# A preamble rebuilt: idle products on TensorE, another order of loads, four weight tiles read where they are converted, scans in halves

## The chip, the cores and the metric

The kernel runs on one core of a Trainium2 chip. Its engines take their own instruction lists in order and wait for each other by semaphores: TensorE (PE in the profile, its weight loads PEld), VectorE (DVE), ScalarE (ACT), GpSimd (POOL) and SyncE (SP), which issues most DMAs. The metric is device microseconds from start to end of one execution, lower is better. The kernel before takes 944.94 us (median of three runs, 944.64 to 945.94).

## The reference

```python
# attention: per batch b and head h a 48x48 state, over 768 time steps
cur = u * k[t] outer v[t];  y[t] = r[t] @ (state + cur)
state = w[t][:, None] * state + k[t] outer v[t]
# x: (4*768 tokens) x 384
h = x @ moe_w_in;  x = (h * clip(h + 3, 0, 6) / 6) @ moe_w_out            # 2048 hidden
xn = x / sqrt(mean(x*x) + 1e-6) * rms_g
out = (silu(xn @ moe2_w_gate) * (xn @ moe2_w_val)) @ moe2_w_out          # 1536 hidden
```

Everything is float32.

## The kernel before

The time axis is cut into 6 chunks of 128 steps, so a chunk has 4 x 128 = 512 tokens. A job is one chunk of one batch (24 jobs); within a job the recurrence is turned into products over 128 steps. The kernel is one stream of steps: for each chunk and each of the 16 tiles of 128 hidden columns ("layers", f) there is one step with a product into the hidden layer (hps, `ff1`), a relu on ACT and a minimum and multiply on DVE (g, `emit_act`), and, one step later, a product back to 384 columns (o, `ff2`). For chunk 0 the first five layers run twice, on columns 0 to 255 of the tokens (jobs 0 and 1) and then on 256 to 511 (jobs 2 and 3), so that jobs 2 and 3 can be made meanwhile: steps 0 to 4 are layers 0 to 4 on the first half, step 5 is layer 0 on the second.

A job of chunk 0 goes through these pieces (methods of `Job`):

- `scans` on DVE: two scans over w (the two halves of the tile), with a reciprocal between them. `muls`: r and k multiplied by what the scans give (rk).
- `pairs` on DVE makes rp, `pe_bonus` multiplies it with u (tile uc) on PE into cps, ACT copies it to cb; `fill` on ACT writes eight tiles a, iperm scaled by cb.
- `pe_a` on PE: the scores aps from rk. `choose` on DVE: where the mask says so, a takes the scores.
- `pe_y0` on PE: yps from v and a; `copy_y0` on ACT puts it into x0, the input of the layers.
- `pe_kt`, `copy_kt`, `pe_u`, `add_u` bring the state up to the next chunk (ktp by transposes with ident, ups, st).

The input weights are stored as 64-bit floats. A `Weight` (one layer's two matrices) is loaded as raw, ACT makes mag from the upper words (`scale`), DVE shifts the lower words (`TENSOR_SCALAR x<-raw`) and joins both (`x<-mag,x`) into a tile x (`bits`), and a DMA copies x to its place in the arena wide_a. For tiles 0 and 1 (`near`) layer products of the first half read x itself; for all others they read wide_a, so they wait for that DMA. raw, x and mag rotate through 3, 3 and 2 buffers; the load of tile f+3 waits until raw f has been read.

The order of work is written by hand. Ahead of the steps a preamble issues the loads and runs jobs 0 and 1 whole and parts of job 2 and of tiles 0 and 1 (the calls of `run` at the end of the set-up). In the steps, the lists `before`, `between` and `behind` say what is issued ahead of a step's first product, between its two products, and after. Each engine takes its instructions in this order; SP does so for DMAs, which move in one queue over 16 DMA engines, and at most eight are issued ahead of the oldest that has not landed, since there are eight DMA semaphores in turn.

Of the kernel before, what the change touches and what calls it, by code (L numbers as in the profile page):

```python
# [28 lines left out]
W1 = 7  # L29
# [7 lines left out]
def kernel(  # L37
# [23 lines left out]
    ps_h = pool(pctx, "ps_h", 2, space=PSUM)  # L61
    ps_s = pool(pctx, "ps_s", space=PSUM)
# [24 lines left out]
    dd = a1_p.tile([128, NP, 2, HF + 1], F32, name="dd")

    st_all = [a1_p.tile([128, 16 + NP * D + 16], F32, name=f"st{b}") for b in range(B)]
    st = [t[:, 16:16 + NP * D].rearrange("p (a d) -> p a d", a=NP) for t in st_all]  # L90
    uc = a1_p.tile([128, NP, 2], F32, name="uc")
    f1 = [a1_p.tile([128, NP, 1], F32, name=f"f1{b}") for b in range(B)]

    def arena(p, name, n):
# [37 lines left out]
    class Weight:  # L132
# [16 lines left out]
        def bits(self):  # L149
            x = st_p.tile([128, 2 * DM], U32, tag="x", name="x", bufs=3)  # L150
            nc.vector.tensor_scalar(x, self.words()[0], 29, None, ALU.logical_shift_right)
            nc.vector.scalar_tensor_tensor(
                out=x, in0=self.mag.bitcast(U32), scalar=3, in1=x, op0=ALU.logical_shift_left, op1=ALU.bitwise_or)
            self.x = x.bitcast(F32).rearrange("p (a n) -> p a n", a=2)
            nc.sync.dma_start(
                out=self.dst[:, :, 1, :].bitcast(U32), in_=x.rearrange("p (a n) -> p a n", a=2))
            if not self.near:
                self.x = self.dst[:, :, 1, :].bitcast(F32)

# [8 lines left out]
    class Piece:  # L168
# [31 lines left out]
        def out(self):  # L200
            hl = de_p.tile([128, 2 * DM], F32R, tag="hl", name="hl", bufs=3)
            h = hl.rearrange("p (l n) -> p l n", l=2)
            nc.scalar.activation(out=h[:, 0, :], in_=self.x, func=AF.Copy)
            nc.gpsimd.tensor_tensor(out=h[:, 1, :], in0=self.x, in1=h[:, 0, :].bitcast(F32), op=ALU.subtract)
            dst = wo_d[self.s] if self.kind == 2 else wp_d[self.j]
            nc.sync.dma_start(out=dst[:, self.f], in_=h.bitcast(F32))
# [57 lines left out]
    class Job:  # L264
# [16 lines left out]
                out=x, data0=x, data1=dd.rearrange("p a h j -> p (a h j)"),  # L281
                initial=0.0, op0=ALU.mult, op1=ALU.add)

        def scans(self):
            nc.vector.memset(dd[:, :, :, 0:1], 1.0)
            self.scan(0)
            self.s1, self.s2 = self.w[:, 0], self.w[:, 1]
            nc.vector.reciprocal(out=dd[:, :, :, 0:1], in_=self.s1[:, :, :, HF:HF + 1])
            self.scan(1)

        def decay(self):
            b = self.b
# [150 lines left out]
            nc.scalar.activation(out=x0[:, :, self.b * CH:(self.b + 1) * CH], in_=self.yps, func=AF.Copy)  # L443


    def emit_h(slot, xt, ps):
        for k in range(KT):
            for j, (l, r) in enumerate(PASS):
                nc.tensor.matmul(  # L449
                    ps, slot[:, l, k * 128:(k + 1) * 128], xt[:, k, r, :],  # L450
                    start=(k == 0 and j == 0), stop=(k == KT - 1 and j == 2))
# [83 lines left out]
    jobs = [Job(c, b) for c in range(NC_) for b in range(B)]  # L535
    wa = [Weight(wa_d[f]) for f in range(F1)]
# [9 lines left out]
    before, between, behind = ([[] for _ in steps] for _ in range(3))  # L546
# [14 lines left out]


    j0, j1, j2, j3 = jobs[:B]
    before[0] += [j2.muls]
    between[0] += [j3.pairs, j2.pe_bonus, j2.fill]
    between[1] += [j2.pe_a, j2.choose, j3.pe_bonus]
    behind[1] += [wa[3].scale, j3.fill, j2.pe_y0, j2.copy_y0, j3.scans]
    before[2] += [j3.muls]
    behind[2] += [j3.pe_a, j3.choose]
    between[3] += [j3.pe_y0, j3.copy_y0]  # L570
    for j, n in enumerate((1, 2, 3, 4)):
        behind[n] += [jobs[j].decay]
        behind[n + 1] += [jobs[j].pe_kt, jobs[j].copy_kt]
# [4 lines left out]
        for b in range(B):  # L578
            plan(c * B + b, first[c] - 18 + 4 * b)

    begun = {f: f - 2 for f in range(2, W1)} | {7: 7, 8: 8} | {f: f + 1 + (f > 13) for f in range(9, F1)}
    for f, n in begun.items():
        if n != 1:
            (behind[n - 1] if n else before[n]).append(wa[f].scale)
        behind[n] += [wa[f].bits]
        if f + 3 < F1:
            behind[n] += [wa[f + 3].load]
    for f in range(F1):
        before[f + 19 if f < F32_F else f + LAGS[0] - 1] += [wa[f].parts]
    behind[2] += [lambda: jobs[4].load("w", "rk", "rks", "v")]  # L590
    behind[4] += [lambda: jobs[5].load("w", "rk", "v")]

    def norm_plan(c, n, last):
# [59 lines left out]
    def run(fs):  # L653
        for x in fs:
            x()
# [297 lines left out]
        return [lambda m=m: one(m) for m in range(KT)]  # L953


    j0.load("w")
    nc.vector.memset(uc, 0.0)
    for i in range(2):
        nc.sync.dma_start(
            out=uc[64 * i:64 * i + D, :, i], in_=u_d.rearrange("o (p i d) -> i d (o p)", p=NP, i=2)[i])  # L960
    j0.load("rk")
    j1.load("rk")
    nc.sync.dma_start(out=iperm, in_=iperm_d)
    j1.load("w")
    nc.sync.dma_start(out=mask, in_=mask_d)
    wa[0].load()
    j0.load("v")
    j1.load("v")
    j2.load("w")
    wa[1].load()  # L970
    j2.load("rk")
    j3.load("rk", "w")
    wa[2].load()
    j2.load("v")
    j3.load("v")
    nc.sync.dma_start(out=ident, in_=ident_d)
    nc.sync.dma_start(out=ub, in_=u_d.to_broadcast([128, DM]))
    nc.sync.dma_start(out=gain, in_=g_d)
    nc.vector.memset(dd, 0.0)
    nc.vector.memset(half, 0.5)  # L980
    nc.vector.memset(eps, 1e-6)
    nc.vector.memset(ones.bitcast(F32), 1.0)
    for t in st_all:
        nc.gpsimd.memset(t, 0.0)
    for f in range(W1):
        wa[f].dst = wpair[f]
        wa[f].near = f < 2
    run((j0.scans, j0.pairs, j0.pe_bonus, j0.muls, j1.pairs, j0.fill, j0.pe_a, wa[0].scale, j1.pe_bonus, j1.fill))
    run((j1.scans, j1.muls, lambda: j1.pe_a(True), j0.choose, j0.pe_y0, wa[0].bits, wa[3].load, j1.choose, j1.pe_y0))
    run((wa[1].scale, wa[1].bits, wa[4].load, j2.pairs, j2.scans, j0.copy_y0, j1.copy_y0))  # L990
    pin()


# [40 lines left out]
    ps_h = pool(ctx, "ps_h1", space=PSUM, reuse_waits="tile")  # L1034
# [106 lines left out]
    for j in range(6 * NG + 1):  # L1141
        p, k = divmod(j, 2 * NG)
# [34 lines left out]
        want, n = {5: 7, 6: 6}.get(j, 9), 0  # L1177
# [107 lines left out]
```

## Time and profile before

| | |
|---|---|
| median of three runs | 944.94 us (944.64 to 945.94) |
| the profiled execution, own time | 944.94 us |
| its span, first to last instruction | 943.1 us |
| PE busy | 927.3 us, 98% |
| DVE, ACT, POOL busy | 644.2 (68%), 476.1 (50%), 534.8 (57%) |
| PE's first product | at 8.70 us |
| HBM read and written | 134.29 and 39.32 MB |
| share of the chain of waits | PE 92%, DVE 3%, DMA 2%, issue 1%, ACT 1%, POOL 1% |

The profile is that of one execution. An engine is busy while an instruction of it runs; what it did ahead of an instruction, and what it waited for, stands in square brackets behind a row of the timeline ("idle before, released by"). The chain of waits is followed back from the last instruction: at each point it names the one thing that was being waited for. Products on PE are in pairs of records where the operands are float32. A granted clock of 1.00 is 2.4 GHz, 0.50 is 1.2; where the trace has no record of it the column shows 1.00.

### The profile page before, as it was taken

Reading aid. Unit: us, or ns where it says so; the run is one execution under the profiler, and the core shown is the slowest. Engines: PE = TensorE matmul, PEld = TensorE weight load, DVE = VectorE, ACT = ScalarE, POOL = GpSimd, SP = SyncE. Lnnn points to the kernel's source line nnn. Section 1 sums busy time; section 2 is a strip of 40 time slices with the busy share of each in tenths; the row PEclk is TensorE's granted clock in tenths of the full one; section 3 lists DMA queues with packets and bytes.
Section 4 is the critical chain, followed back from the end, with each engine's and each line's share of the span. In section 5 each row is a group of like instructions: output and inputs, shape, how many; then the busy total and the mean of one; then the engine's idle time right before and its main releaser. Section 6 shows DMA issues by size and latency. Waiting matters only on the chain.

```text
span 943.1 us, 14286 instructions
## 1 busy us (share of the span) xinstructions
PE 927.3 (98%) x5085; PEld 733.9 (78%) x5085; DVE 644.2 (68%) x913; ACT 476.1 (50%) x946; POOL 534.8 (57%) x454
## 2 busy tenths in 40 slices
PE   5999999999999999999999999999999999999998
PEld 5775578778878887777888888887877878888886
DVE  7777767777778777776545377647988457554555
ACT  3554656546645554655454653446555445433331
POOL 0043255766756776674466677489466679335423
PEclk9999999999999999999999999999999999999999
DMA  9888532246545554652752387764699742644321
GB/s 341 296 310 289 198 136 85 85 149 243 194 132 198 179 169 152 232 177 57 243 195 96 131 308 265 269 242 160 217 376 332 273 158 90 244 167 154 147 79 67
DMA packets 63127, 184.77 MB, mean 196 GB/s; under 512 B 8912, under 2 KB 23248, under 8 KB 58448
## 3 DMA queue, kind: packets, MB, share of 16 engines
q1 hardware_dynamic: 63056, 183.87, 55.0%
q8 instruction: 40, 0.66, 0.3%
q14 instruction: 31, 0.25, 0.1%
HBM read 134.29 MB, written 39.32 MB: 184 GB/s over the span
## 4 chain that ended last, share of the span: by engine, by line
PE 92%; DVE 3%; DMA 2%; issue 1%; ACT 1%; POOL 1%; SPq 0%; POOLq 0%; DVEq 0%
PE o L478 18%; PE hps L449 18%; PE o L762 15%; PE pe L762 10%; PE pc L762 9%; PE pa L762 5%; PE o L461 3%; PE pb L762 3%; PE hps L455 3%; PE aps L361 2%; PE yps L403 2%; PE pd L762 1%; PE yps L397 1%; PE ktp L345 1%; PE ups L376 1%
## 5 line engine op out<-in xcount | busy, mean ns | idle before, releaser
L472 POOL TENSOR_TENSOR g<-a,g 128x512 fp32r<-128x512 f32 x84 | 116.2, 1383 | 146.8 <-ACT g L471 135.7
L467 DVE SCALAR_TENSOR_TENSOR a<-a,hps 128x512 f32<-128x512 f32 x84 | 57.3, 682 | 86.5 <-ACT a L466 85.0
L478 PE MATMUL o<-g,wide_b 128*128 128x512 f32 x441 | 113.3, 399 | 0.0
L449 PE MATMUL hps<-xt,wide_b 128*128 128x512 f32 x441 | 111.9, 398 | 0.0
L762 PE MATMUL o<-xt,wide_b 128*128 128x512 f32 x405 | 107.6, 395 | 0.0
L466 ACT ACTIVATE a<-hps,half 128x512 f32<-128x512 f32 x84 | 57.5, 684 | 92.9 <-PE hps L449 88.5
L449 PEld LDWEIGHTS hps<-xt,wide_b 128*128 128x128 f32 x441 | 82.7, 187 | 21.2 <-issue 1.2
L478 PEld LDWEIGHTS o<-g,wide_b 128*128 128x128 f32 x441 | 81.1, 188 | 19.5 <-issue 0.5
L471 ACT ACTIVATE g<-a 128x512 fp32r<-128x512 f32 x84 | 53.2, 633 | 79.5 <-DVE a L467 77.4
L762 PEld LDWEIGHTS o<-xt,wide_b 128*128 128x128 f32 x405 | 76.0, 188 | 18.2
L478 PE MATMUL o<-g,wide_a 128*128 128x512 f32 x315 | 78.6, 394 | 0.0
L280 DVE TENSOR_TENSOR_SCAN w<-w,dd 128x520 f32<-128x520 f32 x48 | 74.6, 1553 | 5.0 <-DMA w<-in_dram 3.4
L449 PE MATMUL hps<-xt,wide_a 128*128 128x512 f32 x315 | 77.6, 390 | 0.2 <-POOL xt L426 0.2
L449 PEld LDWEIGHTS hps<-xt,wide_a 128*128 128x128 f32 x315 | 59.0, 188 | 13.3 <-POOL xt L426 0.6
L478 PEld LDWEIGHTS o<-g,wide_a 128*128 128x128 f32 x315 | 58.2, 188 | 12.3 <-issue 0.2
L797 DVE TENSOR_TENSOR q<-pc,q 128x512 f32<-128x512 f32 x80 | 55.1, 689 | 17.6 <-PE pc L762 6.7
L338 ACT ACTIVATE a<-iperm,cb 128x128 f32<-128x128 f32 x192 | 58.5, 389 | 0.1
L863 POOL TENSOR_TENSOR q<-q,q 128x512 f32<-128x512 f32 x36 | 49.3, 1368 | 13.5 <-DVE q L797 13.3
L762 PE MATMUL o<-g,wide_b 128*128 128x512 f32 (+1 forms) x216 | 55.5, 390 | 0.0
L307 POOL TENSOR_TENSOR rks<-rks 128x384 f32<-128x384 f32 x20 | 32.8, 1641 | 30.2 <-DMA rks<-in_dram 23.8
L859 ACT ACTIVATE q<-q 128x512 f32<-128x512 f32 x40 | 25.3, 632 | 48.6 <-DVE q L797 48.6
L797 DVE TENSOR_TENSOR q<-pe,q 128x512 f32<-128x512 f32 x40 | 27.6, 689 | 32.1 <-PE pe L762 32.1
(206 smaller groups left out, 2002.9 us busy)
## 6 DMA issues: line engine op xcount, KB each, us to landing
wraw<-in_dram SPq DMA_DIRECT2D x36, 384.0 KB, 4.2
wide_b<-wo SPq DMA_DIRECT2D x12, 1152.0 KB, 8.8
w<-wd SPq DMA_DIRECT2D x10, 1280.0 KB, 6.1
wide_b<-wd SPq DMA_DIRECT2D x10, 1280.0 KB, 6.0
w<-in_dram SPq DMA_DIRECT2D x24, 520.0 KB, 3.8
rk<-in_dram SPq DMA_DIRECT2D x24, 512.0 KB, 4.9
raw<-in_dram SPq DMA_DIRECT2D x16, 768.0 KB, 7.4
rks<-in_dram SPq DMA_DIRECT2D x20, 384.0 KB, 5.5
```

Of the source, the lines that this page charges most:

```text
L280: nc.vector.tensor_tensor_scan(out=x, data0=x, data1=dd.rearrange("p a h j -> p (a h j)"), initial=0.0, op0=ALU.mult, op1=ALU.add)
L307: nc.gpsimd.tensor_tensor(out=x, in0=x, in1=self.rks[:, 1, :], op=ALU.mult)
L338: nc.scalar.activation(out=self.head(h), in_=iperm, func=AF.Copy, scale=self.cb[:, h, :])
L449: nc.tensor.matmul(ps, slot[:, l, k * 128:(k + 1) * 128], xt[:, k, r, :], start=(k == 0 and j == 0), stop=(k == KT - 1 and j == 2))
L466: nc.scalar.activation(out=a, in_=ps, func=AF.Relu, scale=1.0 / 6.0, bias=half)
L467: nc.vector.scalar_tensor_tensor(out=a, in0=a, scalar=1.0, in1=ps, op0=ALU.min, op1=ALU.mult)
L471: nc.scalar.activation(out=g[:, 0, :], in_=a, func=AF.Copy)
L472: nc.gpsimd.tensor_tensor(out=g[:, 1, :], in0=a, in1=g[:, 0, :].bitcast(F32), op=ALU.subtract)
L478: nc.tensor.matmul(acc[m][:, cols], slot[:, l, m * 128:(m + 1) * 128], g[:, r, :], start=(first and j == 0), stop=(parts or last and j == ...
L762: nc.tensor.matmul(ps, lhs[:, l, :], rhs[:, r, :], start=first and j == 0, stop=True, skip_group_check=not (first and j == 0))
L797: nc.vector.tensor_tensor(out=out, in0=a, in1=b, op=op)
L863: eng.tensor_tensor(out=o, in0=src, in1=self.gate.o[i], op=ALU.mult)
```

## The change

- PE gets 42 products of a tile of ones with itself whose result nobody reads (`warm`): 24 first, 8 after the turn of u, 10 ahead of job 1's scores.
- u is no longer gathered by two DMAs of 4-byte pieces on SP; it is loaded as four rows on ACT's queue, turned by one small product with iperm, and copied by ACT in reverse order into uc (`turn_u`). iperm's load moves to ACT's queue too.
- The first job's w is loaded in two halves; w of jobs 2 and 3, v of job 3, ident, ub and gain come later.
- Tiles 2 and 3 are `near` as well: four tiles are read in x. The DMA to wide_a is a method of its own (`out`), and for tiles 0, 1, 3 and 4 stands after the load of a later tile.
- `scans` can be called in halves; the work of jobs 2 and 3 and of tiles 2 to 5 stands at other places in the preamble and in steps 0 to 4.

```diff
         def bits(self):
...
-            nc.sync.dma_start(
-                out=self.dst[:, :, 1, :].bitcast(U32), in_=x.rearrange("p (a n) -> p a n", a=2))
+
+        def out(self):
+            nc.sync.dma_start(out=self.dst[:, :, 1, :].bitcast(F32), in_=self.x)
             if not self.near:
                 self.x = self.dst[:, :, 1, :].bitcast(F32)
...
+    def warm(n):
+        ps = ps_h.tile([128, 128], F32, tag="h", name="warm")
+        for i in range(n):
+            nc.tensor.matmul(ps, ones.bitcast(F32), ones.bitcast(F32), start=True, stop=True)
+
+    def turn_u():
+        ps = ps_s.tile([128, NP], F32, tag="s", name="ups")
+        nc.tensor.matmul(ps, u4[0:NP, :], iperm[0:NP, HF - NP:HF], start=True, stop=True)
+        for i in range(2):
+            t = ps[64 * i:64 * i + 64, NP - 1:NP]
+            back = bass.AP(t.tensor, t.offset, [t.ap[0], (-1, NP)])
+            nc.scalar.activation(out=uc[64 * i:64 * i + 64, :, i], in_=back, func=AF.Copy)
...
-    before[0] += [j2.muls]
-    between[0] += [j3.pairs, j2.pe_bonus, j2.fill]
-    between[1] += [j2.pe_a, j2.choose, j3.pe_bonus]
-    behind[1] += [wa[3].scale, j3.fill, j2.pe_y0, j2.copy_y0, j3.scans]
-    before[2] += [j3.muls]
-    behind[2] += [j3.pe_a, j3.choose]
-    between[3] += [j3.pe_y0, j3.copy_y0]
+    between[0] += [j2.pe_bonus, j2.scan_a]
+    between[1] += [j2.fill, j2.scan_b, j2.muls]
+    between[2] += [j3.pairs, wa[3].scale, wa[3].bits, wa[6].load, wa[3].out]
+    behind[2] += [j2.pe_a, j3.pe_bonus, j2.choose, j3.fill, j3.scan_a]
+    between[3] += [j2.pe_y0, wa[4].scale, j2.copy_y0, j3.scan_b, j3.muls, wa[4].bits, wa[7].load, wa[4].out]
+    behind[3] += [j3.pe_a, j3.choose, wa[5].scale]
+    between[4] += [j3.pe_y0, j3.copy_y0]
...
-    begun = {f: f - 2 for f in range(2, W1)} | {7: 7, 8: 8} | {f: f + 1 + (f > 13) for f in range(9, F1)}
+    begun = {f: f - 2 for f in range(5, W1)} | {7: 7, 8: 8} | {f: f + 1 + (f > 13) for f in range(9, F1)}
...
-    j0.load("w")
+    j0.w = su_p.tile(list(w_d[0].shape), F32, tag="w", name="w", bufs=B)
+    for i in range(2):
+        nc.sync.dma_start(out=j0.w[:, i], in_=w_d[0][:, i])
+    nc.vector.memset(ones.bitcast(F32), 1.0)
...
-    for i in range(2):
-        nc.sync.dma_start(
-            out=uc[64 * i:64 * i + D, :, i], in_=u_d.rearrange("o (p i d) -> i d (o p)", p=NP, i=2)[i])
+    nc.scalar.dma_start(
+        out=u4[0:NP].rearrange("p (i j) -> p i j", i=2)[:, :, 0:D],
+        in_=u_d.rearrange("o (p i d) -> (o p) i d", p=NP, i=2))
+    nc.scalar.dma_start(out=iperm, in_=iperm_d)
...
-        wa[f].near = f < 2
-    run((j0.scans, j0.pairs, j0.pe_bonus, j0.muls, j1.pairs, j0.fill, j0.pe_a, wa[0].scale, j1.pe_bonus, j1.fill))
-    run((j1.scans, j1.muls, lambda: j1.pe_a(True), j0.choose, j0.pe_y0, wa[0].bits, wa[3].load, j1.choose, j1.pe_y0))
-    run((wa[1].scale, wa[1].bits, wa[4].load, j2.pairs, j2.scans, j0.copy_y0, j1.copy_y0))
+        wa[f].near = f < 4
+    warm(24)
+    turn_u()
+    warm(8)
+    run((j0.scan_a, j0.scan_b, j0.pairs, j0.pe_bonus, j0.muls, j1.pairs, j0.fill, j0.pe_a, j1.pe_bonus, j1.fill))
+    warm(10)
+    run((wa[0].scale, j1.scan_a, j1.scan_b, j1.muls, lambda: j1.pe_a(True), j0.choose, j0.pe_y0, j0.copy_y0))
+    run((j1.choose, j1.pe_y0, wa[0].bits, wa[1].scale, wa[3].load, wa[0].out, j1.copy_y0, lambda: j3.load("w")))
+    run((j2.pairs, wa[1].bits, wa[2].scale, wa[4].load, wa[1].out, wa[2].bits, lambda: j3.load("v"), wa[5].load))
```

Three places show what this does to the lists. PE from its first product on, before (cps: bonus products, aps: scores of jobs 0 and 1):

```order
L326 MATMUL cps<-uc,rp 128x2 x4
L361 MATMUL aps<-rk 128x128 x8
L326 MATMUL cps<-uc,rp 128x2 x4
L361 MATMUL aps_250<-rk 128x128
L361 MATMUL aps_251<-rk 128x128
```

and now (warm: idle products, ups<-iperm: the turn of u):

```order
L457 MATMUL warm<-ones 128x128 x24
L461 MATMUL ups<-iperm,u_109 128x4
L457 MATMUL warm<-ones 128x128 x8
L334 MATMUL cps<-uc,rp 128x2 x4
L369 MATMUL aps<-rk 128x128 x8
L334 MATMUL cps<-uc,rp 128x2 x4
L457 MATMUL warm<-ones 128x128 x10
L369 MATMUL aps_294<-rk 128x128
```

The same job products now stand behind 24 + 1 + 8 and 10 others. PE from layer 3's product on the first half to layer 4's, before (hps and o: the two products of a layer, yps: job 3's, ups and ktp: the state's):

```order
L455 MATMUL hps<-x_93,wide_a 128x256 x3
L438 MATMUL yps<-a,v 32x128 x16
L376 MATMUL ups<-v,kt 64x48 x8
L461 MATMUL o_380<-g,wide_a 128x256
L461 MATMUL o_381<-g,wide_a 128x256
L461 MATMUL o_382<-g,wide_a 128x256
L345 MATMUL ktp<-ident,rk 128x128 x4
L455 MATMUL hps<-x_93,wide_a 128x256 x3
```

and now, from job 3's scores to layer 3's o, with layer 4's product as the hps (layer 3's reads x and stands further ahead; the yps is job 3's):

```order
L369 MATMUL aps<-rk 128x128 x8
L353 MATMUL ktp<-ident,rk 128x128 x4
L476 MATMUL hps<-x_93,wide_a 128x256 x3
L446 MATMUL yps<-a,v 32x128 x16
L384 MATMUL ups<-v,kt 64x48 x8
L482 MATMUL o_411<-g,x 128x256
L482 MATMUL o_412<-g,x 128x256
L482 MATMUL o_413<-g,x 128x256
```

Job 3's scores stood ahead of layer 3's product and stand ahead of layer 4's now; its yps stood ahead of layer 4's product and stands behind it. SP where tiles 2 to 4 go home, before (wide_a<-x: copies of tiles 2, 3, 4; raw: loads):

```order
L155 DMA wide_a<-x 128x2x384
L138 DMA raw<-in_dram 128x768
L155 DMA wide_a<-x 128x2x384
L138 DMA raw<-in_dram 128x768
L155 DMA wide_a<-x 128x2x384
L138 DMA raw<-in_dram 128x768
```

and now, for tiles 3 and 4 (the second of the two copies in one row is tile 5's):

```order
L1018 DMA gain<-in_dram 128x3
L139 DMA raw<-in_dram 128x768
L158 DMA wide_a<-x 128x2x384
L139 DMA raw<-in_dram 128x768
L158 DMA wide_a<-x 128x2x384 x2
L139 DMA raw<-in_dram 128x768
```

The load of a later tile stood behind each copy and stands ahead of it for tiles 3 and 4.

## Rows read from the trace of the kernel before

**Rows 1.** The page, its head: the span of the profiled execution.
```profile
span 943.1 us, 14286 instructions
```

**Rows 2.** Busy time by stretch: us, each engine (instructions), granted clock, DMA share, GB/s.
```profile
35.00:943.00 908.00, 903.15 (x4882) 712.74 (x4881) 615.35 (x865) 457.55 (x898) 532.92 (x442) 1.00 0.54 191
```

**Rows 3.** Timeline of PE, 8 to 30 us: start, us, line, operation [idle before].
```profile
8.70 1.87 PE L326 MATMUL cps<-uc,rp 128*128 128x2 f32 x8 [8.70 <-DVE rp L320]
...
14.91 2.08 PE L361 MATMUL aps<-rk 48*128 48x128 f32 x16 [0.54 <-DVE rk L303]
...
23.97 0.95 PE L326 MATMUL cps<-uc,rp 128*128 128x2 f32 x8
```

**Rows 4.** Products of yps, 17 to 20 us and 20.7 to 22.2: ns min/median/max.
```profile
L438 PE MATMUL yps<-a,v x40: 420/421/422, 16.9 to 19.9; 128*32 128x128 f32 x40
...
L438 PE MATMUL yps<-a,v x20: 272/273/397, 20.4 to 21.7; 128*32 128x128 f32 x20
```

**Rows 5.** Timeline of ACT, 10 to 18 us: columns as in rows 3.
```profile
10.61 0.18 ACT L329 ACTIVATE cb<-cps 128x8 f32<-128x8 f32 x1 [8.59 <-PE cps L326]
...
10.81 2.45 ACT L338 ACTIVATE a<-iperm,cb 128x128 f32<-128x128 f32 x8
```

**Rows 6.** Timeline of DVE, 0 to 45 us: columns as in rows 3.
```profile
0.81 0.07 DVE L957 MEMSET uc<- 128x8 f32 x1 [0.81 <-PEq L1273]
...
4.65 1.24 DVE L280 TENSOR_TENSOR_SCAN w<-w,dd 128x520 f32<-128x520 f32 x1 [3.03 <-DMA w<-in_dram]
...
7.96 0.69 DVE L320 TENSOR_TENSOR rp<-rk 128x512 f32<-128x512 f32 x1 [0.55 <-DMA rk<-in_dram]
...
10.92 1.24 DVE L280 TENSOR_TENSOR_SCAN w<-w,dd 128x520 f32<-128x520 f32 x1 [0.32 <-DMA w<-in_dram]
...
16.00 0.55 DVE L151 TENSOR_SCALAR x<-raw 128x768 uint32<-128x768 uint32 x1
...
17.53 1.34 DVE L367 COPY_PREDICATED a<-mask,aps 128x512 f32<-128x512 uint32 x2
...
28.01 0.42 DVE L467 SCALAR_TENSOR_TENSOR g<-g,hps 128x256 f32<-128x256 f32 x1 [0.64 <-ACT g L466]
...
36.77 1.34 DVE L367 COPY_PREDICATED a<-mask,aps 128x512 f32<-128x512 uint32 x2 [1.22 <-PE aps L361]
...
38.01 0.54 DVE L151 TENSOR_SCALAR x<-raw 128x768 uint32<-128x768 uint32 x1
```

**Rows 7.** Chain of waits, 0 to 60 us: start, us, what (x records).
```profile
27.40 5.33 DMA wide_a<-x
...
38.80 1.90 PE yps L438 x32
...
43.23 1.30 PE hps L455 x6
44.53 0.60 PE ups L376 x16
45.13 1.49 PE o L461 x6
46.62 0.44 PE ktp L345 x4
47.06 1.30 PE hps L455 x6
```

**Rows 8.** DMA issues at 24.87, 39.57, 282.1 and 631.6: KB, us to landing.
```profile
raw<-in_dram SPq DMA_DIRECT2D x1, 768.0 KB, 6.9
...
wide_a<-x SPq DMA_DIRECT2D x1, 384.0 KB, 3.0
...
wraw<-in_dram SPq DMA_DIRECT2D x1, 384.0 KB, 3.2
...
w<-wd SPq DMA_DIRECT2D x1, 1280.0 KB, 5.5
```

**Rows 9.** Waits of PE, 21 to 943 us: total, times, longest.
```profile
PE hps L455 <- DMA wide_a<-x: 1.1, 1, 1.1
```

More of the change, by code (lines that the diff above doesn't have):

```diff
@@ L91 @@
     uc = a1_p.tile([128, NP, 2], F32, name="uc")
+    u4 = su_p.tile([128, 128], F32, name="u4")
     f1 = [a1_p.tile([128, NP, 1], F32, name=f"f1{b}") for b in range(B)]
@@ L282, in scan, with scan_a @@
                 initial=0.0, op0=ALU.mult, op1=ALU.add)
-        def scans(self):
+        def scan_a(self):
             nc.vector.memset(dd[:, :, :, 0:1], 1.0)
@@ L288, in scans, with scan_b @@
             nc.vector.reciprocal(out=dd[:, :, :, 0:1], in_=self.s1[:, :, :, HF:HF + 1])
+        def scan_b(self):
             self.scan(1)
+        def scans(self):
+            self.scan_a()
+            self.scan_b()
         def decay(self):
@@ L579 @@
             plan(c * B + b, first[c] - 18 + 4 * b)
-    begun = {f: f - 2 for f in range(2, W1)} | {7: 7, 8: 8} | {f: f + 1 + (f > 13) for f in range(9, F1)}
+    begun = {f: f - 2 for f in range(5, W1)} | {7: 7, 8: 8} | {f: f + 1 + (f > 13) for f in range(9, F1)}
     for f, n in begun.items():
-        if n != 1:
-            (behind[n - 1] if n else before[n]).append(wa[f].scale)
-        behind[n] += [wa[f].bits]
+        if f > 5:
+            behind[n - 1].append(wa[f].scale)
+        behind[n] += [wa[f].bits, wa[f].out]
         if f + 3 < F1:
@@ L589 @@
         before[f + 19 if f < F32_F else f + LAGS[0] - 1] += [wa[f].parts]
-    behind[2] += [lambda: jobs[4].load("w", "rk", "rks", "v")]
+    behind[3] += [lambda: jobs[4].load("w", "rk", "rks", "v")]
     behind[4] += [lambda: jobs[5].load("w", "rk", "v")]
@@ L953, in ff2_units @@
         return [lambda m=m: one(m) for m in range(KT)]
-    j0.load("w")
+    j0.w = su_p.tile(list(w_d[0].shape), F32, tag="w", name="w", bufs=B)
+    for i in range(2):
+        nc.sync.dma_start(out=j0.w[:, i], in_=w_d[0][:, i])
+    nc.vector.memset(ones.bitcast(F32), 1.0)
+    nc.vector.memset(u4, 0.0)
+    nc.vector.memset(dd, 0.0)
+    nc.vector.memset(half, 0.5)
+    nc.vector.memset(eps, 1e-6)
     nc.vector.memset(uc, 0.0)
-    for i in range(2):
-        nc.sync.dma_start(
-            out=uc[64 * i:64 * i + D, :, i], in_=u_d.rearrange("o (p i d) -> i d (o p)", p=NP, i=2)[i])
+    nc.scalar.dma_start(
+        out=u4[0:NP].rearrange("p (i j) -> p i j", i=2)[:, :, 0:D],
+        in_=u_d.rearrange("o (p i d) -> (o p) i d", p=NP, i=2))
+    nc.scalar.dma_start(out=iperm, in_=iperm_d)
     j0.load("rk")
-    j1.load("rk")
-    nc.sync.dma_start(out=iperm, in_=iperm_d)
-    j1.load("w")
+    j1.load("rk", "w")
     nc.sync.dma_start(out=mask, in_=mask_d)
@@ L968 @@
     j1.load("v")
-    j2.load("w")
     wa[1].load()
     j2.load("rk")
-    j3.load("rk", "w")
     wa[2].load()
+    j2.load("w")
+    j3.load("rk")
     j2.load("v")
[L975 to L982, printed above, removed]
     for t in st_all:
@@ L986 @@
         wa[f].dst = wpair[f]
-        wa[f].near = f < 2
-    run((j0.scans, j0.pairs, j0.pe_bonus, j0.muls, j1.pairs, j0.fill, j0.pe_a, wa[0].scale, j1.pe_bonus, j1.fill))
-    run((j1.scans, j1.muls, lambda: j1.pe_a(True), j0.choose, j0.pe_y0, wa[0].bits, wa[3].load, j1.choose, j1.pe_y0))
-    run((wa[1].scale, wa[1].bits, wa[4].load, j2.pairs, j2.scans, j0.copy_y0, j1.copy_y0))
+        wa[f].near = f < 4
[7 more added lines that the diff above has]
+    run((j2.pairs, wa[1].bits, wa[2].scale, wa[4].load, wa[1].out, wa[2].bits, lambda: j3.load("v"), wa[5].load))
+    nc.sync.dma_start(out=ident, in_=ident_d)
+    wa[2].out()
+    nc.sync.dma_start(out=ub, in_=u_d.to_broadcast([128, DM]))
+    nc.sync.dma_start(out=gain, in_=g_d)
     pin()
```

## The prediction

> **What bounds the kernel now.** I read the windows first: after 35 us PE is busy 903.15 us of 908 [rows 2], so from there the time is PE's own work, and a change of the first five layers can only move the moment at which that stretch begins. I take as mark the product of the sixth step (layer 0 on the second half of the tokens), which the chain of waits starts at 47.06 [rows 7]; what PE has behind it is the same list in both kernels. Of the profiled execution's 943.1 us [rows 1] 896.0 lie behind the mark, and they move with it one for one. That execution took 944.94, 1.84 outside the span, and is itself the median of the three runs.
>
> Ahead of the mark the chain is a wait for a copy, 5.33 us for a converted tile to come home to wide_a, and then PE without a gap [rows 7]. The copy was released by DVE at 27.40, and DVE had hardly stopped since 4.65: its pauses until 38.01 are 0.55 (rk), 0.32 (w), 0.64 (a relu of ACT) and 1.22 (products of PE) [rows 6]. So two things race to the mark: DVE's list in its order, and PE's list, which until 20 us runs at half speed. The bonus products of job 0 take 1.87 us at 8.70 and those of job 2 0.95 at 23.97 [rows 3]; the products of yps take 421 ns each up to 19.9 and 272 from 20.4 [rows 4]. The column of the granted clock reads 1.00 over both stretches, so I go by durations: 1.2 GHz until about 20.3, 2.4 after. What PE did before it rose: dense products from 14.91 on [rows 3], 5.4 us.
>
> **The change, part by part.** I walk to the mark through the instructions that wait last.
>
> *Idle products.* They start as soon as ones is written, now DVE's first instruction (its first stood at 0.81 [rows 6]): 1.05, an estimate. Their price stands in no row. From below: half of a product on 256 columns, 1.30 for six records, two to a product [rows 7], so 0.217. From above: a bonus product, with the same weights and two columns, 0.95 for four [rows 3], so 0.238. I take 0.23, near the bonus product whose weight load it shares, and 0.46 at half speed. If the clock rises 5.4 us after dense work begins, as it did from 14.91, it rises at 6.45: 11.7 products by then, the other 12.3 of the 24 in 2.83, until 9.28. The turn of u costs 0.1 (an estimate; its operands come on ACT's queue, and ACT had no work before 10.61 [rows 5]), the next 8 products 1.84. So job 0's bonus products start at 11.2, where before they started at 8.70 [rows 3]. PE takes its list in order, so loads that come earlier don't help them: behind them stand bonus 0.95, scores 1.09 (half of 2.08, about), job 1's bonus 0.95, ten more idle products 2.30, and job 1's scores 1.09: 17.6. ACT's path to the same place is shorter: 11.2 + 0.98 to the bonus, 0.2 for its copy, 2.45 for the fill of job 0 [rows 5], 0.2 and seven eighths of the second fill: 17.2. DVE's choice for job 1 therefore starts at 17.65; before it started at 17.53 [rows 6]. What the order of loads, the two halves of w and the missing u loads win ahead of it (job 0's scan by some 0.7, half a load of w; job 1's by 2) ends here as a wait of DVE.
>
> *DVE's list from that choice to the fifth tile.* Before, from 17.53 to 38.55 (38.01 + 0.54) [rows 6]: 21.02, of which 1.86 were waits, so 19.16. The new order takes out job 3's choice, now behind the fifth tile (36.77 to 38.01: 1.24), and puts in tile 0 (16.00 to 17.53: 1.53) and the minimum of layer 3 (0.42, as at 28.01): 19.9. The halves of the scans and the muls are the same instructions at other places, at no cost of their own. Waits: the 1.22 for job 3's scores goes, since the choice is later; the 0.64 for ACT's relu stays, and I count it twice, since the relu of layer 3 now stands on ACT behind job 3's fill of 2.45. 21.15, so the first half of tile 4's conversion ends at 38.8. Bounds: 19.9 without a wait, 21.8 with all the waits of before.
>
> *Four tiles read where they were converted.* The 5.33 us of [rows 7] go: layers 2 and 3 wait for DVE alone and their products come some 5 us sooner. But tile 4 still goes home by a copy, and PE's order puts layer 4's product ahead of job 3's yps. So PE, done with job 3's scores and four transposes some 1.5 us after DVE's muls, at about 39.8, waits there instead: the wait moves from layer 2 to layer 4. The ident load, queued late now, can hold the first transposes by half a microsecond; this wait covers it.
>
> *The fifth copy.* Before, out followed at once on the conversion and the next load came after it: 3.0 from issue to landing [rows 8]. Now the load of tile 7 is issued when the first half of the conversion has freed the raw tile, and out after the second half, behind it on SP. A load of 768 KB on an idle queue has no row; between 384 KB in 3.2 and 1280 KB in 5.5 [rows 8] it is 4.2. What a copy pays behind a raw load the trace shows at 24.87: that load took 6.9, until 31.8 [rows 8], and the copy issued at 27.40 landed 5.33 later [rows 7], at 32.7, 0.9 behind it. So layer 4 starts at 38.8 + 0.04 + 4.2 + 0.9 + 0.05 = 44.0. From below: out alone, 38.8 + 0.96 (the second half) + 3.0 + 0.05 = 42.8.
>
> *From layer 4 to the mark.* Product 1.30, job 3's yps 1.90 (before, it lay in the wait ahead of this product), ups 0.60, out product 1.49, transposes 0.44 [rows 7]: 5.73, so 49.7 against 47.06, 2.65 later. 944.94 + 2.65 = **947.6**.
>
> **Rivals.** *The products stay out of the way* (the clock rises at once, or a product is cheaper than its neighbours in the rows). Then DVE sets the choice. From 4.65 to 17.53 it has 12.88, less tile 0 (1.53), less the waits for rk and w (0.87): 10.5, from a scan at 3.95 on: 14.4, or 3.2 before my 17.65. The mark is at 46.5, 0.6 sooner than before: **944.4**. For it: PE idles until 8.70 now. Against it: even at full speed from the first product on, PE's list above (32 idle products in 7.4, then 0.95, 1.09, 0.95, ten more in 2.3, and 1.09) ends at 14.9.
>
> *Faster than before: no wait at layer 4.* The same, and the copy lands as if alone (1.25 sooner) and ACT is never late (1.3 sooner): the mark at 44.0, **941.9**. It decides if the first half of tile 4's conversion ends by 34.3. For it: DVE would begin 0.7 sooner and lose 0.87 of waits. Against it: SP's order, and a queue that served load and copy in turn at 24.87.
>
> *The clock is low for longer.* Either it rises late: counted from PE's first product at 8.70 it took 11.6 us [rows 3, 4], not 5.4, and with that all 24 run at half speed and the bonus products start 3 us later, **950.6**. Or it falls again in the wait of some 4 us ahead of layer 4, where the work behind it is on the path: if it takes 5.4 us to rise, 2.7 us are lost, **950.3**. The longest single wait of this kind since the rise was 1.1 us [rows 9], and the products behind it ran at 1.30 to 1.49 for six records [rows 7], the upper level; a longer one no row shows. The Trainium skill (TensorE: Matmul & The Clock Gate, section HAM oscillation — how this bites in real kernels) says that a DMA wait between bursts of matmuls can throttle the array again, so that the next burst starts cold. By that rule this second half of the rival holds; no run here shows it yet.
>
> **How the numbers follow.** Forecast 0.45, products out of the way 0.22, faster 0.13, clock low 0.20. The forecast's own range is 946.3 (DVE's waits gone) to 949.2 (the clock 2 us later, which costs half of that, and all waits of before). A measurement of this kernel can tell 0.2% from no change, 1.9 us: 943.05 and 946.83. Within these lie the second case and about 0.09 of the first, 0.31; faster 0.13; slower 0.56. The range reaches from 943.8, which leaves out the faster case and little more, to 950.3, which leaves out half of the last.
>
> **What would show it.** In the profile after: idle products of 0.46 and then 0.23; bonus products of job 0 waiting for PE's own list, not for DVE; job 1's choice near 17.6; a PE wait of 3 to 4 us ahead of layer 4's product, released by the copy to wide_a, with the raw load issued just ahead; the sixth step's product near 49.7. It is wrong if that wait is under 1 us, if the choice starts before 16, or if anything behind the mark takes another time than before.

## The result, and the profile after

The changed kernel takes 955.12 us (median of four runs, 954.45 to 956.07) against 944.79 for the kernel before (944.50 to 945.94): ratio 1.0109 [1.0097, 1.0121], 10.3 us slower. The forecast was 947.6, slower by 2.65, with a range up to 950.3: the direction was right, the size was not. The ratio is not the quotient of the two medians, so the two can differ by about 0.1%. The profiled execution of the changed kernel, from which all rows of it are read, took 956.07 us and is the slowest of its four.

The head of the page [rows 1], then the busy time by stretch: us, each engine (instructions), granted clock, DMA share, GB/s [rows 2].

```profile
span 954.3 us, 14467 instructions
```

```profile
7.00:34.10 27.10, 24.01 (x234) 21.96 (x233) 23.28 (x37) 15.95 (x47) 0.37 (x2) 1.00 1.00 375
34.30:40.90 6.60, 5.53 (x34) 4.28 (x36) 1.41 (x3) 1.88 (x3) 0.08 (x1) 0.50 0.46 179
41.10:47.70 6.60, 4.55 (x52) 3.50 (x48) 5.13 (x9) 3.13 (x5) 0.00 (x0) 1.00 0.51 169
47.90:54.60 6.70, 5.63 (x35) 4.23 (x36) 1.89 (x4) 0.47 (x1) 0.00 (x0) 0.50 0.83 299
...
54.70:942.00 887.30, 885.61 (x4746) 697.84 (x4745) 602.32 (x846) 453.24 (x891) 530.28 (x442) 1.00 0.54 188
```

From 54.7 on PE is busy 885.61 of 887.30, as before. Ahead of that the clock falls twice to 0.50, which is 1.2 GHz. PE's timeline tells what stood before each fall (start, us, line, operation, [idle before]; warm are the idle products, cps the bonus products, ktp the first transposes, hps a layer's product, yps job 2's at 38.95 and job 3's at 51.83):

```profile
1.05 8.38 PE L457 MATMUL warm<-ones 128*128 128x128 f32 x48 [1.05 <-DVE ones L980]
...
11.56 0.95 PE L334 MATMUL cps<-uc,rp 128*128 128x2 f32 x8
...
35.37 1.09 PE L353 MATMUL ktp<-ident,rk 128*128 128x128 f32 x4 [3.78 <-DMA ident<-in_dram]
36.25 2.77 PE L476 MATMUL hps<-x,x 128*128 128x256 f32 x6
38.95 2.93 PE L446 MATMUL yps<-a,v 128*32 128x128 f32 x32
...
48.97 2.93 PE L476 MATMUL hps<-x,wide_a 128*128 128x256 f32 x6 [3.33 <-DMA wide_a<-x]
51.83 3.31 PE L446 MATMUL yps<-a,v 128*32 128x128 f32 x32
...
57.50 1.46 PE L476 MATMUL hps<-x,wide_a 128*128 128x256 f32 x6
```

The same view of before has the first transposes and the mark at:

```profile
36.65 0.66 PE L345 MATMUL ktp<-ident,rk 128*128 128x128 f32 x4
...
46.89 1.46 PE L455 MATMUL hps<-x,wide_a 128*128 128x256 f32 x6
```

PE now waits 3.78 us for ident and 3.33 us for the copy of tile 4; behind each wait its products take nearly twice their time (layer 3's 2.77, layer 4's 2.93, where 1.46 stands at the sixth step). The sixth step's product, the mark, starts at 57.50 in this view; in the same view of before it started at 46.89 (47.06 in the chain [rows 7]). The gap is 10.6, and from the mark to the end of the span it is 896.8 us against 896.2.

DVE's timeline (rows that answer to [rows 6]):

```profile
18.12 1.36 DVE L375 COPY_PREDICATED a<-mask,aps 128x512 f32<-128x512 uint32 x2 [1.82 <-PE aps L369]
...
39.56 0.42 DVE L488 SCALAR_TENSOR_TENSOR g<-g,hps 128x256 f32<-128x256 f32 x1 [5.19 <-ACT g L487]
...
42.23 0.55 DVE L152 TENSOR_SCALAR x<-raw 128x768 uint32<-128x768 uint32 x1
```

DVE, which hardly stopped before, stands still for 5.19 us: the minimum of layer 3 (39.56) needs layer 3's product, which stands on PE behind the transposes that wait for ident. So the late load holds DVE too, and with it the conversion of tile 4 (42.23). Where ident was shows in SP's own list and in the DMA issues (KB, us to landing):

```profile
12.43 0.33 SPq L277 DMA_DIRECT2D v<-in_dram  x1
19.99 0.33 SPq L139 DMA_DIRECT2D raw<-in_dram  x1
...
24.78 0.56 SPq L139 DMA_DIRECT2D raw<-in_dram  x1
25.39 0.44 SPq L1015 DMA_DIRECT2D ident<-in_dram  x1
```

```profile
raw<-in_dram SPq DMA_DIRECT2D x1, 768.0 KB, 10.3
ident<-in_dram SPq DMA_DIRECT2D x1, 64.0 KB, 9.8
```

And before:

```profile
15.69 0.33 SPq L976 DMA_DIRECT2D ident<-in_dram  x1
```

```profile
ident<-in_dram SPq DMA_DIRECT2D x1, 64.0 KB, 9.9
```

SP issued nothing from 12.8 to 20.0: the fourth raw load waited for DVE to free a raw tile. Then three raw loads, two copies, w and v of job 3 and behind them ident were all issued within 5.8 us. Ident, 64 KB, took 9.84 us behind them and landed at 35.23. In the kernel before it was issued at 15.69, ahead of all that, and landed at 25.6. It took as long there (9.9): what has changed is the moment of issue, 9.7 us later, and the moment at which PE comes to the transposes, some 5 us sooner.

### The profile page after: what moved, and what is told of

It is laid out like the page before. It is cut to its first block, busy times and chain, and to the rows that moved or that the text cites. A ratio compares the mean times of both kernels' runs of the same rounds, so it can differ in the third digit from the quotient of the medians.

```text
span 954.3 us, 14467 instructions
## 1 busy us (share of the span) xinstructions
PE 940.7 (99%) x5171; PEld 745.5 (78%) x5171; DVE 642.5 (67%) x914; ACT 476.1 (50%) x948; POOL 532.6 (56%) x454
## 4 chain that ended last, share of the span: by engine, by line
PE 93%; DVE 2%; DMA 2%; ACT 1%; issue 1%; POOL 1%; SPq 0%; POOLq 0%; DVEq 0%
PE o L499 18%; PE hps L470 17%; PE o L783 15%; PE pe L783 10%; PE pc L783 9%; PE pa L783 4%; PE hps L476 3%; PE pb L783 3%; PE o L482 3%; PE aps L369 2%; PE yps L411 2%; PE pd L783 1%; PE warm L457 1%; PE yps L405 1%; PE ktp L353 1%; DMA ident<-in_dram 1%
```

## The experiments

Fourteen kernels, timed in groups (1 to 4, 5 to 8, 9 to 12, 13 and 14). Before was timed again beside each group, so a run is told by its median over that of before. These medians of before lie between 943.55 and 944.13, and at 944.79 beside after; a step between runs of different groups is uncertain by about as much as they differ. Marks are of one profiled execution each. Before's, 46.89, belongs to an execution of 944.94: for an execution as long as its medians beside the groups the mark would be at 45.5 to 46.1, an estimate with the same 1.84 us outside the span and 896.2 behind the mark.

| run | over before, us | ratio and interval | mark |
|---|---|---|---|
| after | +10.33 | 1.0109 [1.0097, 1.0121] | 57.50 |
| 1 ident early | +6.77 | 1.0072 [1.0057, 1.0087] | 51.63 |
| 2 and copies first | +4.83 | 1.0051 [1.0032, 1.0070] | 50.94 |
| 3 waits filled | +7.01 | 1.0085 [1.0066, 1.0105] | 51.93 |
| 4 no idle products | +11.26 | 1.0120 [1.0105, 1.0136] | 54.90 |
| 5 run 2, wait filled | +1.93 | 1.0025 [1.0008, 1.0042] | 47.99 |
| 6 run 2, yps ahead | +1.38 | 1.0007 [0.9996, 1.0019] | 47.91 |
| 7 run 6, 24 idle | +1.64 | 1.0011 [1.0000, 1.0022] | 46.17 |
| 8 before, idle products | +1.64 | 1.0016 [1.0001, 1.0032] | 47.02 |
| 9 run 6, 24, 2, 6 idle | +1.35 | 1.0015 [0.9998, 1.0032] | 45.42 |
| 10 run 6, none idle | +2.32 | 1.0027 [1.0015, 1.0039] | 47.43 |
| 11 before, ident late | +0.15 | 1.0001 [0.9992, 1.0011] | 47.34 |
| 12 before, four near | -0.29 | 0.9997 [0.9988, 1.0006] | 46.04 |
| 13 run 12, 14 and 8 idle | +0.91 | 1.0011 [0.9998, 1.0024] | 46.84 |
| 14 run 1, wait filled | +4.28 | 1.0046 [1.0030, 1.0062] | 49.49 |

**Run 1: ident early.**

```diff
     j2.load("v")
+    nc.sync.dma_start(out=ident, in_=ident_d)
...
-    nc.sync.dma_start(out=ident, in_=ident_d)
     wa[2].out()
```

> Change against after: the load of ident is issued behind v of job 2, ahead of the fourth raw load, and no longer behind the sixth raw load. Theory (the late ident is the larger part of the miss): PE's wait of 3.78 us ahead of the first transposes goes, the transposes run near 31.6 and not at 35.37, layer 3's product near 32.3, DVE's second scan of job 3 some 4.5 us sooner, the sixth step's product near 53 if the clock still falls in the wait ahead of layer 4 (950.5 us), near 50 if it does not fall (947.7). Rival (something else is as late as ident, such as the converted tile 3 or job 3's operands): PE waits at the same place for it, under 1 us is gained, 954 or more. Rival (the idle products set the pace from 18 us on): again 954 or more.

Measured +6.77, 3.6 us less than after (5.9 by the marks, of which 1.15 is job 1's choice, at 16.97 in this execution and at 18.12 in after's). Its PE timeline:

```profile
30.71 0.66 PE L353 MATMUL ktp<-ident,rk 128*128 128x128 f32 x4 [0.27 <-ACT cb L337]
31.20 1.46 PE L476 MATMUL hps<-x,x 128*128 128x256 f32 x6
...
43.25 2.93 PE L476 MATMUL hps<-x,wide_a 128*128 128x256 f32 x6 [4.69 <-DMA wide_a<-x]
46.11 3.15 PE L446 MATMUL yps<-a,v 128*32 128x128 f32 x32
```

The first wait and the first fall of the clock are gone; the second stays, its wait longer (4.69), since PE now comes to it sooner. The transposes ran at 30.71 (31.6 expected, with the choice 1.15 later), and the 1.2 GHz behind the wait is the branch "if the clock still falls" (950.5 expected, 950.32 measured, beside a before of 943.55). That ident is the larger part of the miss is not settled: it is 3.6 of 7.7 us by the medians, and 4.7 of 8.0 by the marks without the choice.

**Run 2: and the copies of tiles 3 and 4 ahead of the raw loads.**

```diff
-    between[2] += [j3.pairs, wa[3].scale, wa[3].bits, wa[6].load, wa[3].out]
+    between[2] += [j3.pairs, wa[3].scale, wa[3].bits, wa[3].out, wa[6].load]
...
-    between[3] += [j2.pe_y0, wa[4].scale, j2.copy_y0, j3.scan_b, j3.muls, wa[4].bits, wa[7].load, wa[4].out]
+    between[3] += [j2.pe_y0, wa[4].scale, j2.copy_y0, j3.scan_b, j3.muls, wa[4].bits, wa[4].out, wa[7].load]
```

> Change against after: ident early as in the first run, and the copies of tiles 3 and 4 to wide_a are issued ahead of the raw loads of tiles 6 and 7. Theory (the copy of tile 4 lands behind the raw load that stands ahead of it on SP): the copy lands about 3 us after it is issued, layer 4 starts some 1.5 to 2 us sooner than in the first run, 948.5 to 949. Rival (queues serve load and copy in turn, the order of issue counts for nothing): the same as the first run within 0.3 us.

1.9 less than run 1, by the medians and from job 1's choice to the mark (34.66 us in run 1, 32.76 in run 2). The copy's issue in run 1 (first line, 38.32) and in run 2 (second fence, 39.53):

```profile
wide_a<-x SPq DMA_DIRECT2D x1, 384.0 KB, 4.9
```

```profile
wide_a<-x SPq DMA_DIRECT2D x1, 384.0 KB, 3.0
```

Behind the raw load the copy takes 1.9 us longer. The Trainium skill (DMA: Bandwidth & Descriptors, section Two DMAs through the same engine are not ordered) says that descriptors within one queue of a DMA engine start in order; the traces agree, with 4.9 behind the load and 3.0 ahead of it.

**Run 3: idle products in both waits of PE, ident as late as in after.**

```diff
-    behind[2] += [j2.pe_a, j3.pe_bonus, j2.choose, j3.fill, j3.scan_a]
+    behind[2] += [j2.pe_a, j3.pe_bonus, j2.choose, j3.fill, j3.scan_a, lambda: warm(16)]
...
+    behind[3] += [lambda: warm(14)]
```

> Change against after: 16 idle products more on PE ahead of the first transposes, and 14 more ahead of layer 4's product, in the two waits in which PE now stands; nothing else moves. Theory (the clock falls in these waits and the half speed behind them costs as much as the rows show): granted clock 1.00 from 7 us on, transposes 0.66 and not 1.09, layer 3's product 1.46 and not 2.77, so layer 4 starts 1.7 us sooner, and 5.7 us and not 8.5 from layer 4 to the sixth step: 4.5 us less, 950.6. Rival (the waits alone cost, and PE at half speed stands in slack): 954 to 955. Rival (idle products do not hold the clock, or start so late that they delay the work): 955 or more.

3.3 less than after, mark 51.93; the granted clock by stretch:

```profile
7.00:34.00 27.00, 26.42 (x257) 24.45 (x257) 23.54 (x38) 16.14 (x47) 0.56 (x3) 1.00 1.00 374
34.00:41.00 7.00, 7.00 (x80) 5.81 (x80) 3.92 (x6) 3.64 (x6) 0.00 (x0) 1.00 0.41 153
41.00:48.00 7.00, 6.13 (x60) 5.39 (x57) 3.00 (x5) 1.73 (x3) 0.00 (x0) 1.00 0.83 277
```

With PE busy through the waits there is no fall. The same late loads then cost 3.3 us less by the medians, 4.9 by the marks (5.57 less 0.7 for an earlier choice): that is the price of the clock, on either side of the 4.5 expected.

**Run 4: no idle products at all.**

```diff
-    warm(24)
     turn_u()
-    warm(8)
...
-    warm(10)
```

> Change against after: the 42 idle products are left out, the turn of u stays. Theory (they cost and give back about the same): the clock rises near 20 us as before, bonus products of job 0 start 2 us sooner but run at half speed, job 1's choice between 16.5 and 17.5 and not at 18.1; ident and the wait ahead of layer 4 stay, so 953.5 to 955.5. Rival (the products hold up PE's list and are the cause of the loss): 3 us less, 952 or under. Rival (without them the whole early part runs at half speed): 957 or more.

0.9 more than after, which the two intervals cannot tell from the same. The 42 products are not what made the kernel slow. (The mark, 54.90, is of the fastest of this run's four executions, 953.28.) Here ident held the transposes for 1.95 us only, and the clock fell behind that wait too: layer 3's product took 2.77.

**Run 5: run 2, with the wait ahead of layer 4 filled.**

```diff
+    behind[3] += [lambda: warm(12)]
```

> Change against the second run (ident early, copies ahead of raw loads; 4.8 us over before): 12 idle products more on PE in the wait ahead of layer 4's product, which the copy to wide_a sets. Theory (the fall of the clock in that wait costs what the rows at either level show): granted clock 1.00 from 7 us to the end, layer 4's product 1.46 and not 2.93, job 3's yps 1.97 and not 3.17, so 2.7 us less: 2.1 us over before, 0.22%. Rival (the half speed lies in slack, or the products hold up layer 4): 4.5 us or more over before.

1.93 against 2.1 expected. Layer 4's product takes 1.56 from 42.16, yps 1.97, and the mark is at 47.99, 5.83 behind layer 4's start.

**Run 6: run 2, with job 3's yps ahead of layer 4's product.**

```diff
-    between[4] += [j3.pe_y0, j3.copy_y0]
+    behind[3] += [j3.pe_y0, j3.copy_y0]
```

> Change against the second run: job 3's yps and their copy stand ahead of layer 4's product on PE and ACT, in the wait for the copy of tile 4, and not behind it. Theory (PE's order put 1.9 us of ready work behind a wait, and that wait let the clock fall): yps run from 40.8 to 42.7, the wait left is under 1.5 us, the clock stays up, and the sixth step's product starts near 46.4, 0.6 ahead of before's: 0.3 us over before to 0.7 under. Rival (only the 1.9 us are won, the clock falls all the same): 2.5 to 3 us over before. Rival (layer 4 is then held by job 3's choice on DVE): 2 us over before or more.

Layer 4's wait for the copy is gone without idle products (it starts at 43.98, the moment yps end, which themselves wait 0.42 and 0.20 for job 3's choice), but the time is 1.38 over before, not 0.3 or less. In the profiled execution, 946.28 long, the clock was low from 15.1 to 18.5, among the ten idle products, and job 1's choice stood at 19.60, not 18.1. The executions range from 944.00 to 947.08.

**Runs 7, 9 and 10: run 6 with 24, with 24, 2 and 6, and with no idle products.**

```diff
     warm(24)
     turn_u()
-    warm(8)
...
-    warm(10)
```

In run 9 these two are warm(2) and warm(6), in run 10 warm(24) goes too. The expectations of runs 7, 9 and 10, in this order:

> Change against the run with yps ahead: of the 42 idle products only the first 24 are left; the 8 behind the turn of u and the 10 ahead of job 1's scores go. Theory (these 18 stand on the path: DVE waits 1.8 us for job 1's scores behind them): job 1's choice near 16 and not at 18.1, everything up to layer 4 some 1.8 us sooner, 1.5 to 2 us less than the run with yps ahead, so 1 to 2 us under before. Rival (the raw loads then set the pace, being issued by what frees their buffers): within 0.5 us of the run with yps ahead. Rival (without them the clock falls between the first products): slower than that run.

> Change against the run with yps ahead: of the 42 idle products 24, 2 and 6 are left, as many as fit into the waits of 0.44 and 1.31 us in which PE stood there with 24 alone. Theory (in that run the clock fell from 12.7 to 19.5 for want of these products, which made yps 4.89 and not 3.35): granted clock 1.00 from 7 to 940 us, job 1's choice near 15.5, the sixth step's product near 44.5, 1.5 to 2.5 us under before. Rival (whether the clock falls early is a matter of where in the program it rises, not of these products): it still falls, within 1 us of the runs with 42 and with 24 products (945.5 and 945.8 beside 944.1).

> Change against the run with yps ahead: all 42 idle products go. Theory (without them the clock rises late, at 18 us, and stays; the first layer's product at 21.3 as in the earlier run without products, and from there to the sixth step's product 24.55 us as in the run with yps ahead): 45.8, 1.2 us ahead of before's, 0.5 to 1.5 us under before. Rival (idle products pay): slower than the run with yps ahead, 1.4 us over before or more.

All three theories missed: 1.64, 1.35 and 2.32 over before. The times are those of rivals: runs 7 and 9 cannot be told from run 6, and run 10 lies 0.9 above it. In the runs with 24 products the clock fell at 12.7 and 12.8; run 9 by stretch:

```profile
7.00:12.70 5.70, 5.70 (x56) 5.43 (x55) 4.84 (x8) 2.16 (x9) 0.19 (x1) 1.00 1.03 398
12.80:16.20 3.40, 3.40 (x19) 3.18 (x20) 2.79 (x5) 3.37 (x13) 0.00 (x0) 0.50 1.02 414
16.30:34.00 17.70, 16.85 (x178) 14.77 (x175) 15.70 (x26) 11.11 (x29) 0.38 (x2) 1.00 1.02 371
```

PE was busy for all of 5.70 us, and the clock fell. In run 10, without idle products, it rose only at 20.9, and job 0's bonus products waited for iperm and the turn of u (9.62, not 8.70 as in [rows 3]): mark 47.43.

**Run 8: before, with the idle products and the turn of u put in** (and, not shown here, the loads of u and iperm on ACT's queue).

```diff
+    warm(24)
+    turn_u()
+    warm(8)
...
+    warm(10)
```

> The kernel before, with only the idle products (24, 8 and 10), the turn of u, and u and iperm loaded on ACT's queue put into it; order of loads, of steps and of layers as before. Forecast's theory (the products set job 1's choice, and DVE's list from there is as long as before): choice near 18.1 and not 17.5, the sixth step's product 0.6 later, 0.3 to 1 us over before. Rival (the higher clock from 7 us on shortens the way to the first layer): 0.5 us or more under before. Rival (idle products are what made the changed kernel slow): 5 us or more over before.

1.64 over; job 1's choice at 18.42, the mark at 47.02, 0.13 behind before's in the profiled execution. The price of the preamble alone is not settled better than that: between 0.1 and 1.6 us.

**Run 11: before, ident issued behind the sixth raw load.**

```diff
-    nc.sync.dma_start(out=ident, in_=ident_d)
...
+    behind[0] += [lambda: nc.sync.dma_start(out=ident, in_=ident_d)]
```

> The kernel before, with one line moved: the load of ident is issued behind the sixth raw load, as in after, and not behind v of job 3. Theory (the late load costs after so much because its first transposes stand at 31.6 there; before's first transposes start at 36.65): it lands between 31 and 36, no wait for it, the same as before within 0.5 us. Rival (a load that late costs 3 us or more wherever the transposes are): 947 or more.

No difference. Ident was issued at 29.40, took 6.6 us and landed near 36.0, later than in after (35.23), and the transposes ran at 36.88 without a wait for it. The same late load is free there, because in before's order they stand 5 us later.

**Runs 12 and 13: before with four tiles read where converted; then with idle products only in PE's idle time.**

```diff
-        wa[f].near = f < 2
+        wa[f].near = f < 4
```

Run 13 has this and:

```diff
+    warm(14)
...
-    run((j1.scans, j1.muls, lambda: j1.pe_a(True), j0.choose, j0.pe_y0, wa[0].bits, wa[3].load, j1.choose, j1.pe_y0))
+    run((j1.scans, j1.muls, lambda: warm(8), lambda: j1.pe_a(True), j0.choose, j0.pe_y0, wa[0].bits, wa[3].load, j1.choose, j1.pe_y0))
```

> The kernel before, with one number changed: four tiles and not two are read where they were converted. Theory (the wait of 5.33 us for the copy of tile 2 is on the chain, but PE has only 1.07 us to win, since its products ahead end at 31.7): the third layer's product at 31.7, the sixth step's 1.1 us sooner, 0.7 to 1.3 us under before. Rival (DVE's list sets the pace behind it): within 0.3 us of before. Rival (the two more tiles keep buffers of x longer and DVE waits for them): slower.

> The kernel before with four tiles read where they were converted (the run before this: 0.3 us under before), and with 14 idle products from the start and 8 ahead of job 1's scores, as many as fit into the time in which PE stands idle there; u loaded as before. Theory (the idle products of the changed kernel cost because they stand on PE's path, not as such): bonus products of job 0 near 8.4 as without them, granted clock 1.00 from 7 us on, yps 3.35 and not 5.07, the first layer's product 1 to 1.7 us sooner and the sixth step's product with it: 1 to 2 us under before. Rival (DVE's list sets the pace up to layer 3): within 0.4 us of the run without them, 0.3 under before. Rival (the clock falls again between these products and the runs spread over 3 us, as all runs with idle products did): a median 0.5 to 1.5 us over before.

Run 12 came to 0.3 under before, which cannot be told from no change, as the first rival said, though its third layer started at 31.20 and not at 32.77. Its mark, 46.04, is 0.3 behind the 45.8 at which before's would be in an execution of median length. Run 13 is 0.91 over, as its last rival said: its clock rose at 4.0, fell at 10.8 and stayed low until 21.1, with PE busy throughout (by stretch):

```profile
4.10:10.80 6.70, 4.42 (x45) 4.03 (x43) 6.07 (x9) 1.83 (x7) 0.19 (x1) 1.00 0.98 371
10.90:21.00 10.10, 10.10 (x84) 9.14 (x85) 9.04 (x16) 5.15 (x15) 0.19 (x1) 0.50 1.03 414
```

None of the fourteen is faster than before by more than can be measured.

**Run 14: the kernel that the forecast took after to be.** Run 1 with 18 idle products in the wait ahead of layer 4.

```diff
+    behind[3] += [lambda: warm(18)]
```

> Change against after: ident early as in the first run, and 18 idle products in the wait ahead of layer 4's product; the copy of tile 4 stays behind the raw load. This is the kernel as the forecast took it to be: no wait for ident, the clock held in the wait. Forecast: 2.65 us over before (0.28%). By the sum of the runs (1.93 over before with the copy ahead, and 1.94 for the copy behind the load): 3.9 over before (0.41%), layer 4's product 1.46 long and near 43.5. If it comes out at 5.5 or more, a cost is missing from both.

4.28 over before by the medians. Its PE timeline:

```profile
43.66 1.56 PE L476 MATMUL hps<-x,wide_a 128*128 128x256 f32 x6 [0.57 <-DMA wide_a<-x]
45.15 1.97 PE L446 MATMUL yps<-a,v 128*32 128x128 f32 x32
...
49.49 1.46 PE L476 MATMUL hps<-x,wide_a 128*128 128x256 f32 x6
```

The mark is at 49.49, 2.60 behind before's 46.89; the forecast said 2.65. The time does not agree as well: of the 1.7 us between 4.28 and 2.60, 0.8 lie behind the mark (897.0 us, not 896.2), and 0.9 come from before's profiled execution, which is that much slower than its median beside this run (944.94, 944.02).

## Why the prediction failed

By its own steps:

- **Idle products: right.** 24 of them took 8.38 us and ended at 9.43 (9.28 predicted), bonus products started at 11.56 (11.2), job 1's choice at 18.12 (17.65), released by PE's scores. The clock rose at 6.9 in this execution (6.45); in the other profiles with 24 products, between 4.3 and 7.1, and where it then held, in after's order, the choice stands between 16.97 and 18.18.
- **DVE's list: right within 1 us** where nothing else stops it. Run 14: choice at 17.47, first half of tile 4 done at 37.73, 20.3 against 21.15.
- **Four near tiles: the step that failed.** The wait did move from layer 2 (its product now starts at 26.76) to layer 4, 3.33 us long where 3 to 4 were predicted. But "The ident load, queued late now, can hold the first transposes by half a microsecond; this wait covers it" is wrong in both halves. It held them by 3.78, because SP, held up by a raw load that waited for DVE, issued it only at 25.39, behind loads that were all issued together. And the wait ahead of layer 4 does not cover it: that wait is set by DVE's conversion of tile 4, and layer 3's product, for which DVE waits, stands behind the transposes.
- **The fifth copy: mis-sized by 0.8 to 1 us.** A raw load on an idle queue took 4.9 (run 1), not 4.2, and from the end of the first half of the conversion to layer 4 it was 6.2 in after, 6.0 in run 1, where 5.19 was said. Run 2 gave 4.1 for the copy ahead, where the lower bound said 4.0. This and DVE's shorter list (0.9) cancel, so that run 14's mark agrees is in part luck.
- **From layer 4 to the mark: right at 2.4 GHz**, 5.83 in runs 5 and 14 (5.73 predicted); at 1.2 GHz 8.53. This was the second half of the rival "the clock is low for longer", priced at 2.7, with a chance of 0.20 for both halves together; it is 2.70 here, and 2.9 by the medians of runs 2 and 5. The Trainium skill (TensorE: Matmul & The Clock Gate, section HAM oscillation — how this bites in real kernels) says that a wait for a DMA between bursts of matmuls throttles the array; the trace agrees, twice, behind waits of 3.78 and 3.33 us, and run 3, in which PE was busy there, has no fall.
- **Behind the mark: 896.8, not 896.2** as in the same view of before, where the forecast had the two equal; run 14 has 897.0, runs 8, 11 and 12 on before's order 896.2 to 896.3. The new order as such is not the cause: runs 2, 5, 6 and 10, which issue the copies ahead of the raw loads, have 896.3 to 896.5; after and runs 1, 3, 4 and 14, which issue them behind, have 896.6 to 897.1. Part of it comes late: near 622 us in run 1 a group of three products starts 0.97 us after the one before it, and 0.69 in run 2. Why is open. In runs 7 and 9, with 896.8 and 897.2, a wait of job 4's yps behind the mark is 0.86 and 0.78 and not 0.30.

After's mark stands 8.01 behind run 14's (57.50, 49.49): 0.65 from the choice (18.12, 17.47), 4.40 from there to the conversion of tile 4 (ident's wait and the half speed behind it: 24.11 us against 19.71), 0.26 from there to layer 4, and 2.70 from layer 4 to the mark. With run 14's 2.60 that is all of the 10.6 between the two profiled executions. By the medians, one edit after another, the 10.33 is 3.56 for ident (run 1), 1.94 for the copies behind the raw loads (run 2), 2.90 for the clock ahead of layer 4 (run 5) and 1.93 that no run takes apart. The forecast had the ident load at 0.5, covered, and the clock as a rival; both happened, and the ident wait made the clock fall once more.

The versions with early marks (runs 7 and 9, 0.7 and 1.5 ahead of before's) are not faster by the median. Most of that lies in what is compared. Beside their groups an execution of before of median length would have its mark at 46.1 and 45.8 (the estimate above), and theirs, 46.17 and 45.42, belong to executions that are among their fastest (944.82 of 944.82 to 946.70; 944.41 of 943.98 to 951.48). That a typical execution of theirs has a later mark is likely and not shown.

## What to carry to other kernels

When a change brings work forward on one engine, list every load that this work reads and follow each through the issuing queue, with the waits of the instructions ahead of it: the smallest and least suspicious one, 64 KB, cost a third of this loss. A later wait covers an earlier one only if what ends the later wait does not hang on the earlier; here DVE's conversion, which ended the later one, waited for a product behind the earlier. Price the time behind a wait of TensorE at half speed (here it fell behind waits of 1.95 to 4.69 us), and look for ready products to move into the wait: in run 6 they kept the clock up there as idle products did in run 5.

## What the runs showed of the hardware

- The clock fell although PE was busy: after 5.70 us of idle, bonus and score products without a pause (run 9). It stayed at 0.50 over 10.10 us of busy PE in run 13. With all 42 idle products it held until waits of 3.78 us in after, 4.69 in run 1 and 2.78 in run 2, held throughout in runs 3, 5, 8 and 14, and fell early in run 6. What tells these apart, no run shows.
- The column of the granted clock shows 1.00 until the first rise is recorded: run 10 has 1.00 from 7 to 20.8 us, and its yps products, from 17.24 on, take 5.07 us for 64 records, not 3.35. The durations tell the level.
- The 64 KB of ident took 9.84 us from issue to landing in after, 9.9 in before and 6.6 in run 11: the size is the same, what was under way when it was issued is not. A raw load of 768 KB took 4.9 on an idle queue (run 1) and 10.3 as the last of the three issued ahead of ident (after).
